# Sink attention and a folded feed-forward on one core: sink values by one full matmul, sink scores behind the score pairs, last tile in three parts

## The chip, the core and the metric

The kernel runs on one core of one Trainium2 chip. The metric is device time in microseconds (us), taken over the whole program. Three runs of the kernel before took 199.46, 199.68 and 200.15 us; their median is 199.68.

## What is computed

Four batches of eight heads, 768 positions, head width 64. Each position attends to the first four positions (the sink) and to a window of 128 positions that ends at itself. The result, as 3072 rows of 512, goes through a feed-forward layer in which two projections are multiplied.

```python
scores = scale * np.matmul(q, k.transpose(0, 1, 3, 2))
is_sink = pos[None, :] < n_sink                 # n_sink = 4
in_window = (rel >= 0) & (rel < window)         # window = 128
a = softmax(np.where(is_sink | in_window, scores, -1e9))
x = np.matmul(a, v).transpose(0, 2, 1, 3).reshape(B * S, H * D)
out = ((x @ w1) * (x @ w2)) @ w3 @ w_out        # 512 -> 1024 -> 1024 -> 512
```

## The kernel before

Everything is bf16 on TensorE, with sums in fp32. The product w3 @ w_out is formed once (`fold_w3`, `fold_mm`, lines 399 to 441), so that each row of output costs the two gate projections and one projection with the folded matrix.

**Attention.** Queries and keys must stand with the head width on the partitions. Batches 0 and 1 get that from TensorE (`transposes`, line 195, the tile `tp`, evacuated by DVE); batches 2 and 3 from transposing transfers that SP issues (`transposes_dma`, line 205). A head pair r and a stage t (two blocks of 128 queries, t = 0, 1, 2) make a unit: `scores` (line 250, tile `sc`) runs four or six matmuls of 64 rows, two heads beside each other on the array; ACT takes the exponential (line 261), DVE multiplies by the window's mask (line 265), and `values` (line 330, tile `av`) runs full-array matmuls with the masked weights as stationary operand. Its last column is the row sum, which DVE divides by (lines 350 and 353). Units are issued in pairs, since the second one of a pair is asked for first thing behind the lead. Batch 0 has units by block in its first two stages (`block_scores`, `block_values`). The results are transposed into `xT` by TensorE (tile `xt`) for batches 0 and 1, and by SP's transfers for 2 and 3.

**The sink.** A query block far from the start still needs the four sink positions. `sink_keys` (line 210) puts the four keys of each head into a block-diagonal operand `ksbd`, so that all eight heads' sink scores come out of four matmuls that each use 32 columns of the array (`sink_scores`, line 232, tile `sp`, once for each batch and each of the stages 1 and 2); ACT writes their exponentials to `es`. `sink_values` (line 222) brings the four sink rows of v to rows 32 * (h // 2) + 4 * (h % 2) of `vs`, so that one matmul for each head pair and block adds the sink's part to `av`. It does so with eight matmuls, one for each head, of four contraction rows each and 64 columns; the stationary operand is a shifted piece of a wide identity matrix, `shifts`. ACT evacuates the result (line 229).

**Feed-forward.** `gate` (line 379, tile `pg`) runs four matmuls for w1 (half 0, evacuated by ACT to `a_sb`) and four for w2 (half 1, multiplied by `a_sb` on DVE into `ab`), for chunks of 256 tokens in batch 0 and of 384 in the others. `project` (line 443, tile `po`) runs eight matmuls for 128 tokens, ACT copies the result (line 451), and SP writes it out (line 454). The very last tile is cut into two halves of 256 columns, the second of which ACT writes itself.

**What sets the order.** The order on TensorE, ACT, DVE and SP is written out while the program is built. Every piece of work is a task with a priority, an estimated time on each engine, the tasks that must be done or begun ahead of it, and the loads that it needs (lines 510 to 642). A planner (lines 645 to 763) keeps an estimated clock for each engine. At each step it takes for TensorE the task that can start first, and among those that can start at once the one of lowest priority number; the other engines take what is ready first. Score pairs are paced: the next may not start until `PACE[b]` us behind the one before (line 649). Where the planner sees TensorE idle early on, it puts in warming matmuls (`keep_busy`, line 457). Once the program is built the order is fixed; an instruction that is not ready holds up its engine. Tiles in PSUM come from two pools, two slots for scores and four for the rest. Loads of q, k and v are issued by POOL in a fixed order, at most eight at a time, and cast to bf16 on their way.

Of the kernel before, what the change touches and what calls it, by code (L numbers as in the profile page):

```python
# [21 lines left out]
def kernel(  # L22
# [31 lines left out]
    XPOSE = (2, 3)  # L54
    BLOCKS = ((0, 0), (0, 1))
    X_XPOSE = (2, 3)
    SPLIT = 6
# [9 lines left out]

    IPAD = P - 4
# [96 lines left out]
    nc.vector.memset(idle[:], 0.0)  # L165
    nc.vector.memset(shifts[:], 1.0)
    nc.vector.memset(maskt[:], 1.0)
    for b in range(B - 1):
        nc.vector.memset(ksbd[b][:], 0.0)

    nc.gpsimd.affine_select(shifts[:], shifts[:], compare_op=ALU.is_equal, fill=0.0,
                            base=-IPAD, pattern=[[1, IPAD + P]], channel_multiplier=-1)

# [43 lines left out]

    def sink_row(h):

        return 32 * (h // 2) + 4 * (h % 2)  # L220

    def sink_values(b):

        vp = ps_mm.tile([P, H, D], FP32, tag="mm", name="vp")
        for h in range(H):
            nc.tensor.matmul(vp[:, h, :], shifts[0:4, IPAD - sink_row(h):IPAD - sink_row(h) + P], vN[b][0:4, 0, h, 0:D],  # L226
                             start=(h == 0), stop=(h == H - 1))
        yield
        nc.scalar.copy(vs[b][:, :, 0:D], vp[:])
        yield  # L230

    def sink_scores(b, t):

        sp = ps_mm.tile([P, 256], FP32, tag="mm", name="sp")
        for r in range(NP):
            rows = slice(32 * r, 32 * r + 32)
            nc.tensor.matmul(sp[rows, :], ksbd[b][:, r * P + 32 * r:r * P + 32 * r + 32],  # L237
                             qT[b][:, r, t * 256:(t + 1) * 256], start=True, stop=True)
        yield
        nc.scalar.activation(es[b][:, (t - 1) * 256:t * 256], sp[:], ACTF.Exp, scale=scale)  # L240
        yield


# [199 lines left out]
    def project(b, m, n0, n1):  # L443

        po = ps_mm.tile([P, n1 - n0], FP32, tag="mm", name="po")
        for kk in range(KFF):
            nc.tensor.matmul(po[:], ab[b][:, kk, m * P:(m + 1) * P], w3o[:, kk, n0:n1],  # L447
                             start=(kk == 0), stop=(kk == KFF - 1))
        yield
        o_sb = w3_sb[:, (b * NB + m) % KFF, 2 * n0:2 * n1].bitcast(FP32)  # L450
        nc.scalar.copy(o_sb, po[:])  # L451
        yield
        t0 = b * S + m * P
        (nc.scalar if n0 else nc.sync).dma_start(out=out[t0:t0 + P, n0:n1], in_=o_sb)
        yield
# [73 lines left out]
    for i in range(KFF):  # L529
        for h in range(2):  # L530
            j0, j1 = 4 * h, 4 * h + 4
            needs = [need("w3", i, x) for x in range(j0 // 4, j1 // 4)]
            task(("t3", i, h), 100 + i + (5 if i < SPLIT and h else 0), fold_w3(i, j0, j1),
                 [("pe", 0.055 * (j1 - j0)), ("dve", 0.05 + 0.075 * (j1 - j0))],
                 [x for a, _ in needs for x in a], [x for _, a in needs for x in a],
                 started=[("t3", i, 0)] if i >= SPLIT and h else [folded(i - SPLIT)] if i >= SPLIT else [], ring="mm")
# [16 lines left out]
    for b in range(B):  # L553
        for t in range(NT):
# [3 lines left out]
            for kb in kbs:  # L558
                if b in XPOSE:
                    for n, src, dst in (("k", kN[b], kT[b]), ("q", qN[b], qT[b])):  # L560
                        qk.append(("td" + n, b, kb))
                        task(qk[-1], 1, transposes_dma(src, dst, kb), [("sp", 1.4), ("dma", XP_US)],
                             war, [(n, b, kb)])
                else:
                    qk.append(("tpk", b, kb))
                    task(qk[-1], 1, transposes(b, kb), [("pe", 0.48), ("dve", 0.65)],
                         war, [("k", b, kb), ("q", b, kb)], "mm")
            if t == 0:
                task(("sk", b), 0, sink_keys(b), [("dve", 0.2)], [("sc", b, 1, 0)])
                task(("sv", b), 2, sink_values(b), [("pe", 0.3), ("act", 0.5)],  # L570
                     [("av", b - 2, NP - 1, NT - 1), ("av", b, 1, 0)] if b >= 2 else [], [("v", b, 0)], "mm")
            else:
                task(("ss", b, t), 2, sink_scores(b, t), [("pe", 0.25), ("act", 0.4)],
                     qk + [("sk", b)], ring="mm")
            if (b, t) in BLOCKS:
                parts = [(j, r0, r0 + 2, [2 * i + r0 // 2]) for i, j in enumerate(kbs) for r0 in (0, 2)]
                if t == 0:
                    parts = [(0, 0, NP, [0, 1])] + parts[2:]
                for u, (j, r0, r1, avs) in enumerate(parts):
                    task(("sc", b, u, t), 4, block_scores(b, j, r0, r1),  # L580
                         [("pe", 0.3), ("act", 1.05), ("dve", 0.7)],
                         [("tpk", b, kb) for kb in (j - 1, j) if kb >= 0], ring="sc", paced=True,
                         started=([unit[-1][0]] if unit else []) + (unit[-4][1] if len(unit) > 3 else []))
                    for a in avs:
                        task(("av", b, a, t), 3, block_values(b, j, 2 * (a % 2)),
                             [("pe", 0.15 if j == 0 else 0.29 if j == 1 else 0.37), ("dve", 0.55)],
                             [("sc", b, u, t)] + ([("ss", b, t), ("sv", b)] if t else []),
                             [("v", b, j)], "mm", last_av)
                        last_av = [("av", b, a, t)]
                    unit.append((("sc", b, u, t), [("av", b, a, t) for a in avs]))  # L590
                    if avs[-1] % 2:
                        task(("xt", b, 2 * (j % 2), t), 2.5, block_x_transposes(b, j),
                             [("pe", 0.24), ("act", 0.6)],
                             [("av", b, avs[-1] - 1, t), ("av", b, avs[-1], t)], [], "mm")
                continue
            for r in range(NP):
                after = list(qk)
                if b >= 2 and t == 0:
                    after.append(("g", b - 2, len(CHUNKS[b - 2]) - 1, KFF - 1, 1))
                lead = r % 2 == 0  # L600
                task(("sc", b, r, t), 4 if lead else 0, scores(b, r, t),
                     [("pe", 0.22), ("act", 0.83), ("dve", 0.58)] if t == 0 else
                     [("pe", 0.28), ("act", 1.05), ("dve", 0.7)], after, ring="sc",
                     slots=2 if lead else 1, paced=lead,
                     started=([unit[-1][0]] if unit else []) + (unit[-3][1] if lead and len(unit) > 3 else []))
                task(("av", b, r, t), 3, values(b, r, t),
                     [("pe", 0.2 if t == 0 else 0.37), ("dve", 0.55)],
                     [("sc", b, r, t)] + ([("ss", b, t), ("sv", b)] if t else []),
                     [("v", b, kb) for kb in kbs], "mm", last_av)
                last_av = [("av", b, r, t)]  # L610
                unit.append((("sc", b, r, t), last_av))
                if not lead and b not in X_XPOSE:
                    task(("xt", b, r - 1, t), 2.5, x_transposes(b, r - 1, t),
                         [("pe", 0.24), ("act", 0.6)],
                         [("av", b, r - 1, t), ("av", b, r, t)], [], "mm")
# [5 lines left out]
    for b in range(B):  # L621
        for c, (t0, t1) in enumerate(CHUNKS[b]):
            last_t = (t1 - 1) // 256
            us = 0.01 + 0.65 * (t1 - t0) / 384
            for dt in range(KFF):
# [10 lines left out]
            for m in range(t0 // P, t1 // P):  # L636
                for n0 in (0, DM // 2) if (b, m) == (B - 1, NB - 1) else (0,):
                    n1 = n0 + DM // 2 if (b, m) == (B - 1, NB - 1) else DM
                    task(("p", b, m) + ((n0,) if n0 else ()), 1300 + 200 * b + m + n0 / 1000,
                         project(b, m, n0, n1),  # L640
                         [("pe", 1.75 * (n1 - n0) / DM), ("act", 0.6 * (n1 - n0) / DM), ("act", 0.1) if n0 else ("sp", SP_US)],
                         [("g", b, c, KFF - 1, 1), *[folded(i) for i in range(KFF)]], ring="mm")
# [77 lines left out]
    while len(done) < len(tasks):  # L720
# [21 lines left out]
        if e == "pe":  # L742
# [55 lines left out]
```

## Time and profile before

| | |
|---|---|
| median of three runs | 199.68 us |
| the profiled execution, its time and its span | 200.22 us, 198.5 us |
| DVE, ACT and POOL, share of the span | 56%, 54%, 38% |
| gate matmuls (line 386), TensorE busy | 91.5 us |
| projection matmuls (line 447), TensorE busy | 42.9 us |
| sink scores (line 237), sink values (line 226), TensorE busy | 2.3 us, 1.6 us |
| granted TensorE clock | 1.000 |
| share of 16 DMA engines' span, POOL's queue and SP's queue | 88.5%, 37.7% |

A row of the chain of waits has the start in us from the beginning of the span, the length in us, the engine, the tile and line, and how many instructions were joined. A row of the groups has line, engine, operation, what is written and read with the shapes, then the count, then busy time in us and mean ns of one, then the idle time just before and what ended it. A row of DMA issues ends with the time from issue to landing in us. "PE" is TensorE's matmuls, "PEld" its weight loads, "SPq" and "ACTq" are transfers issued by SyncE and ScalarE.

### The profile page before, as it was taken

The numbers are of one execution on the slowest core, as the hardware profiler recorded it, in microseconds if no ns is written. First come the engines' busy times: TensorE is split into PE (matmuls) and PEld (weight loads), VectorE is DVE, ScalarE is ACT, GpSimd is POOL, SyncE is SP. The second block draws the span as 40 slices with busy tenths as digits, with TensorE's granted clock in tenths as the row PEclk, the third lists the DMA queues.
The fourth block names the chain that finished last, engine by engine and source line by source line (L and its number), as shares of the span: only waits on it lengthen the run. The fifth ranks groups of instructions, "written<-read, shape, count | busy, mean of one in ns | idle before, by whom it ended". The sixth has DMA issues, their size and how long they took to land.

```text
span 198.5 us, 4533 instructions
## 1 busy us (share of the span) xinstructions
PE 190.3 (96%) x1803; PEld 118.9 (60%) x1815; DVE 111.8 (56%) x262; ACT 107.8 (54%) x179; POOL 75.9 (38%) x102
## 2 busy tenths in 40 slices
PE   7799999989999999999999999999999999999993
PEld 2345566968875786675666656665664565654442
DVE  5544487845786767577668748777781044440000
ACT  2234658634756777975755576667652433333332
POOL 5189967669899962733573300000000000000000
PEclk9999999999999999999999999999999999999999
DMA  5999999999999999999999999950203510002333
GB/s 138 398 387 182 180 159 196 196 160 154 155 144 184 211 144 106 178 158 183 124 144 146 126 156 186 197 110 2 51 5 90 182 48 2 0 3 104 142 141 141
DMA packets 105301, 28.35 MB, mean 143 GB/s; under 512 B 95168, under 2 KB 99776, under 8 KB 105280
## 3 DMA queue, kind: packets, MB, share of 16 engines
q0 software_dynamic: 79648, 12.33, 88.5%
q1 hardware_dynamic: 25488, 15.60, 37.7%
q8 instruction: 14, 0.23, 0.5%
q10 hardware_dynamic: 144, 0.13, 0.2%
q14 instruction: 7, 0.06, 0.1%
HBM read 29.36 MB, written 6.29 MB: 180 GB/s over the span
## 4 chain that ended last, share of the span: by engine, by line
PE 76%; DMA 17%; POOL 4%; SPq 1%; issue 1%; ACT 0%
PE pg L386 39%; PE po L447 21%; DMA w_sb<-in_moe_w_dram 7%; PE av L346 6%; DMA qN<-in_q_dram 5%; PE sc L256 5%; DMA ab<-in_moe_w_dram 4%; PE tp L200 2%; POOL qN L108 1%; POOL vN L108 1%; PE xt L362 1%; SPq L155 1%; POOL kN L108 1%; PE sp L237 1%; PE vp L226 1%
## 5 line engine op out<-in xcount | busy, mean ns | idle before, releaser
L386 PE MATMUL pg<-xT,w_sb 128*128 128x384 bf16 (+1 forms) x576 | 91.5, 308 | 0.0
L386 PEld LDWEIGHTS <-w_sb 128*128 128x128 bf16 x576 | 53.0, 98 | 25.5 <-issue 1.7
L390 DVE TENSOR_TENSOR ab<-a_sb,pg 128x384 bf16<-128x384 f32 (+1 forms) x72 | 36.5, 507 | 32.7 <-PE pg L386 26.2
L393 ACT COPY a_sb<-pg 128x384 f32<-128x384 f32 (+1 forms) x72 | 32.0, 444 | 34.6 <-PE pg L386 17.0
L447 PE MATMUL po<-w3o,ab 128*128 128x512 bf16 (+1 forms) x192 | 42.9, 370 | 0.4
L261 ACT ACTIVATE ex<-sc 128x1024 bf16<-128x1024 f32 (+1 forms) x40 | 37.8, 964 | 6.0 <-PE sc L256 4.1
L447 PEld LDWEIGHTS <-ab 128*128 128x128 bf16 x200 | 19.1, 98 | 20.4 <-issue 0.5
L451 ACT COPY w_sb<-po 128x512 f32<-128x512 f32 (+1 forms) x25 | 14.2, 568 | 25.6 <-PE po L447 25.5
L108 POOL DMA_DIRECT2D qN<-in_q_dram x24 | 22.3, 928 | 14.5 <-DMA vN<-in_v_dram 12.5
L265 DVE TENSOR_TENSOR am<-ex,maskt 128x1024 bf16<-128x1024 bf16 (+1 forms) x40 | 25.6, 645 | 3.6 <-ACT ex L261 3.4
L108 POOL DMA_DIRECT2D kN<-in_k_dram x24 | 22.0, 916 | 7.5 <-DMA qN<-in_q_dram 5.2
L108 POOL DMA_DIRECT2D vN<-in_v_dram x24 | 22.1, 922 | 6.4 <-DMA kN<-in_k_dram 4.5
L353 DVE TENSOR_TENSOR xn<-av,rec 128x256 bf16<-128x256 f32 x40 | 17.0, 424 | 1.4
L346 PE MATMUL av<-vN,am 128*128 128x65 bf16 x296 | 16.8, 193 | 0.0
L346 PEld LDWEIGHTS <-am 128*128 128x128 bf16 x296 | 14.4, 97 | 2.8 <-issue 0.3
L350 DVE RECIPROCAL rec<-av 128x4 f32<-128x4 f32 x40 | 7.2, 179 | 10.7 <-PE av L346 10.4
L202 DVE COPY kqT<-tp 128x1024 bf16<-128x1024 bf16 x12 | 8.3, 690 | 6.3 <-PE tp L200 6.3
L256 PE MATMUL sc<-kqT 64*128 64x128 bf16 (+1 forms) x216 | 11.6, 238 | 0.0
L346 PE MATMUL av<-vs,es 128*128 128x130 bf16 x56 | 11.1, 221 | 0.0
L256 PEld LDWEIGHTS <-kqT 64*128 64x128 bf16 x216 | 6.9, 94 | 3.2 <-issue 2.2
L433 PE MATMUL ph<-wo_sb,w3t 128*128 128x512 bf16 x31 | 7.9, 379 | 0.9 <-ACT wo_sb L413 0.6
L281 ACT ACTIVATE ex<-sc 128x1024 bf16<-128x1024 f32 x7 | 7.1, 1035 | 2.1 <-PE sc L277 2.1
(68 smaller groups left out, 135.6 us busy)
## 6 DMA issues: line engine op xcount, KB each, us to landing
out_dram<-w_sb SPq DMA_DIRECT2D x23, 256.0 KB, 2.2
kN<-in_k_dram POOLq DMA_DIRECT2D x24, 128.0 KB, 7.7
qN<-in_q_dram POOLq DMA_DIRECT2D x24, 128.0 KB, 8.1
vN<-in_v_dram POOLq DMA_DIRECT2D x24, 128.0 KB, 8.0
w_sb<-in_moe_w_dram POOLq DMA_DIRECT2D x9, 256.0 KB, 8.4
ab<-in_moe_w_dram SPq DMA_DIRECT2D x3, 512.0 KB, 6.3
ab<-in_moe_w_out_dram SPq DMA_DIRECT2D x3, 512.0 KB, 7.2
kN<-in_moe_w_dram SPq DMA_DIRECT2D x1, 512.0 KB, 9.4
```

Of the source, the lines that this page charges most:

```text
L108: nc.gpsimd.dma_start(out=dst, in_=rows(src, b, kb))
L202: nc.vector.tensor_copy(kqT[b][:, :, :, kb * P:(kb + 1) * P], tp[:])
L256: nc.tensor.matmul(sc[:, e, c:c + n], kT[b][hp, r, kb * P:(kb + 1) * P], qT[b][hp, r, qb * P:qb * P + n], start=True, stop=True)
L261: nc.scalar.activation(ex[:, :, c0:], sc[:, :, c0:], ACTF.Exp, scale=scale)
L265: nc.vector.tensor_mul(am[:, :, c0:], ex[:, :, c0:], mk)
L346: nc.tensor.matmul(o, lhs, rhs, start=(n == 0), stop=(n == len(todo) - 1), skip_group_check=True)
L353: nc.vector.tensor_mul(xns[b, t][:, :, r, :, :], av[:, :, :, 0:D], rec[:].to_broadcast([P, 2, 2, D]))
L386: nc.tensor.matmul(pg[:], w_sb[:, kk, dt * P:(dt + 1) * P], xT[b][:, kk, tk], start=(kk == 0), stop=(kk == NP - 1))
L390: nc.vector.tensor_mul(ab[b][:, dt, tk], gate_a.pop((b, c, dt))[:], pg[:])
L393: nc.scalar.copy(a_sb[:], pg[:])
L447: nc.tensor.matmul(po[:], ab[b][:, kk, m * P:(m + 1) * P], w3o[:, kk, n0:n1], start=(kk == 0), stop=(kk == KFF - 1))
L451: nc.scalar.copy(o_sb, po[:])
```

## The change

Sink values: one matmul of 128 contraction rows and 512 columns with `pick`, a matrix that copies each of the four sink rows to the eight places of the heads, so that every place gets all heads; DVE then multiplies by `ones_s`, the mask that keeps each head's own four rows. `shifts` becomes a plain identity.

Sink scores: the task now has priority -1 and may start once the second unit of the stage's first score pair has begun. Batch 1 (`SINKS`) makes both stages' sink scores with one group of 512 columns. In the planner's estimates a change of the array's shape is priced (`TURN`), the times of tasks on TensorE are set anew, and the pace of batch 2 is 3.5 in place of 5 and of batch 3 5.5 in place of 4.5.

Last tile: three parts of 256, 128 and 128 columns. ACT copies the first and the last, DVE the middle one; SP writes the first two, ACT the last.

```diff
+    SINKS = (1,)
...
-    shifts = const.tile([P, IPAD + P], BF16, name="shifts")
-    ident = shifts[:, IPAD:IPAD + P]
+    ident = const.tile([P, P], BF16, name="ident")
+    pick = const.tile([P, P], BF16, name="pick")
...
+    pk = pick[:].rearrange("p (r x) -> p r x", x=32)
+    for e in range(2):
+        nc.gpsimd.tensor_copy(pk[:, :, 4 * e:4 * e + 4],
+                              ident[:, 0:4].rearrange("p (r s) -> p r s", r=1).to_broadcast([P, NP, 4]))
...
         vp = ps_mm.tile([P, H, D], FP32, tag="mm", name="vp")
-        for h in range(H):
-            nc.tensor.matmul(vp[:, h, :], shifts[0:4, IPAD - sink_row(h):IPAD - sink_row(h) + P], vN[b][0:4, 0, h, 0:D],
-                             start=(h == 0), stop=(h == H - 1))
-        yield
-        nc.scalar.copy(vs[b][:, :, 0:D], vp[:])
+        nc.tensor.matmul(vp[:], pick[:], vN[b][:, 0, :, 0:D], start=True, stop=True)
+        yield
+        nc.vector.tensor_mul(vs[b][:, :, 0:D], vp[:],
+                             ones_s[:].rearrange("p (h o) -> p h o", o=1).to_broadcast([P, H, D]))
...
-    def sink_scores(b, t):
+    def sink_scores(b, t0, t1):
-        sp = ps_mm.tile([P, 256], FP32, tag="mm", name="sp")
+        sp = ps_mm.tile([P, (t1 - t0) * 256], FP32, tag="mm", name="sp")
...
-                             qT[b][:, r, t * 256:(t + 1) * 256], start=True, stop=True)
+                             qT[b][:, r, t0 * 256:t1 * 256], start=True, stop=True)
...
-        nc.scalar.copy(o_sb, po[:])
+        (nc.vector.tensor_copy if n0 == DM // 2 else nc.scalar.copy)(o_sb, po[:])
...
-        (nc.scalar if n0 else nc.sync).dma_start(out=out[t0:t0 + P, n0:n1], in_=o_sb)
+        (nc.scalar if n0 > DM // 2 else nc.sync).dma_start(out=out[t0:t0 + P, n0:n1], in_=o_sb)
...
-                task(("ss", b, t), 2, sink_scores(b, t), [("pe", 0.25), ("act", 0.4)],
-                     qk + [("sk", b)], ring="mm")
+                if b not in SINKS:
+                    task(("ss", b, t), -1, sink_scores(b, t, t + 1), [("pe", 0.12), ("act", 0.4)],
+                         qk + [("sk", b)], ring="mm", started=[] if (b, t) in BLOCKS else [("sc", b, 1, t)])
+                elif t == 1:
+                    more = [(n, b, kb) for n in (("tdk", "tdq") if b in XPOSE else ("tpk",)) for kb in (4, 5)]
+                    task(("ss", b, 1), -1, sink_scores(b, 1, NT), [("pe", 0.225), ("act", 0.6)],
+                         qk + more + [("sk", b)], ring="mm", started=[("sc", b, 1, 1)])
...
-                for n0 in (0, DM // 2) if (b, m) == (B - 1, NB - 1) else (0,):
-                    n1 = n0 + DM // 2 if (b, m) == (B - 1, NB - 1) else DM
+                cuts = (0, DM // 2, 3 * DM // 4, DM) if (b, m) == (B - 1, NB - 1) else (0, DM)
+                for n0, n1 in zip(cuts, cuts[1:]):
...
-    PACE = [0.0, 3.4, 5, 4.5]
-    last_sc = 0.0
+    PACE = [0.0, 3.4, 3.5, 5.5]
+    TURN, SHAPE = 0.095, {"sc": 1, "ss": 2}
+    last_sc, shape = 0.0, 0
...
+            if SHAPE.get(k["name"][0], 0) != shape:
+                shape = SHAPE.get(k["name"][0], 0)
+                us += TURN
```

More of the change, by code (lines that the diff above doesn't have):

```diff
@@ L165 @@
     nc.vector.memset(idle[:], 0.0)
-    nc.vector.memset(shifts[:], 1.0)
+    nc.vector.memset(ident[:], 1.0)
     nc.vector.memset(maskt[:], 1.0)
+    nc.vector.memset(pick[:], 0.0)
     for b in range(B - 1):
         nc.vector.memset(ksbd[b][:], 0.0)
-    nc.gpsimd.affine_select(shifts[:], shifts[:], compare_op=ALU.is_equal, fill=0.0,
-                            base=-IPAD, pattern=[[1, IPAD + P]], channel_multiplier=-1)
+    nc.gpsimd.affine_select(ident[:], ident[:], compare_op=ALU.is_equal, fill=0.0,
+                            base=0, pattern=[[1, P]], channel_multiplier=-1)
     m4 = maskt[:].rearrange("p v (a c q) -> p (v a) c q", c=2, q=P)
@@ L237, in sink_scores @@
             nc.tensor.matmul(sp[rows, :], ksbd[b][:, r * P + 32 * r:r * P + 32 * r + 32],
-                             qT[b][:, r, t * 256:(t + 1) * 256], start=True, stop=True)
+                             qT[b][:, r, t0 * 256:t1 * 256], start=True, stop=True)
         yield
-        nc.scalar.activation(es[b][:, (t - 1) * 256:t * 256], sp[:], ACTF.Exp, scale=scale)
+        nc.scalar.activation(es[b][:, (t0 - 1) * 256:(t1 - 1) * 256], sp[:], ACTF.Exp, scale=scale)
         yield
@@ L565 @@
                     qk.append(("tpk", b, kb))
-                    task(qk[-1], 1, transposes(b, kb), [("pe", 0.48), ("dve", 0.65)],
+                    task(qk[-1], 1, transposes(b, kb), [("pe", 0.45), ("dve", 0.65)],
                          war, [("k", b, kb), ("q", b, kb)], "mm")
@@ L585 @@
                         task(("av", b, a, t), 3, block_values(b, j, 2 * (a % 2)),
-                             [("pe", 0.15 if j == 0 else 0.29 if j == 1 else 0.37), ("dve", 0.55)],
-                             [("sc", b, u, t)] + ([("ss", b, t), ("sv", b)] if t else []),
+                             [("pe", 0.125 if j == 0 else 0.245 if j == 1 else 0.36), ("dve", 0.55)],
+                             [("sc", b, u, t)] + ([("ss", b, 1 if b in SINKS else t), ("sv", b)] if t else []),
                              [("v", b, j)], "mm", last_av)
@@ L601 @@
                 task(("sc", b, r, t), 4 if lead else 0, scores(b, r, t),
-                     [("pe", 0.22), ("act", 0.83), ("dve", 0.58)] if t == 0 else
-                     [("pe", 0.28), ("act", 1.05), ("dve", 0.7)], after, ring="sc",
+                     [("pe", 0.17), ("act", 0.83), ("dve", 0.58)] if t == 0 else
+                     [("pe", 0.225), ("act", 1.05), ("dve", 0.7)], after, ring="sc",
                      slots=2 if lead else 1, paced=lead,
@@ L606 @@
                 task(("av", b, r, t), 3, values(b, r, t),
-                     [("pe", 0.2 if t == 0 else 0.37), ("dve", 0.55)],
-                     [("sc", b, r, t)] + ([("ss", b, t), ("sv", b)] if t else []),
+                     [("pe", 0.187 if t == 0 else 0.36), ("dve", 0.55)],
+                     [("sc", b, r, t)] + ([("ss", b, 1 if b in SINKS else t), ("sv", b)] if t else []),
                      [("v", b, kb) for kb in kbs], "mm", last_av)
@@ L623 @@
             last_t = (t1 - 1) // 256
-            us = 0.01 + 0.65 * (t1 - t0) / 384
+            us = 0.65 * (t1 - t0) / 384
             for dt in range(KFF):
```

16 lines of the change are left out of this document (7 added, 9 removed).

## Prediction

> **What bounds the kernel now.** I read, from coarse to fine, the page's engine totals, the chain that ended last in order of time, TensorE's timeline where the chain reaches it, and one window over the long stretch behind that.
>
> ```profile
> PE 190.3 (96%) x1803; PEld 118.9 (60%) x1815; DVE 111.8 (56%) x262; ACT 107.8 (54%) x179; POOL 75.9 (38%) x102
> ...
> 33.70 10.39 DMA qN<-in_q_dram
> ...
> 195.34 0.37 ACT w_sb L451
> ```
>
> ```profile
> 43.37 0.40 PE L200 MATMUL tp<-shifts,kN 128*128 128x128 bf16 x4 [0.23 <-DMA kN<-in_k_dram]
> 44.14 0.40 PE L200 MATMUL tp<-shifts,qN 128*128 128x128 bf16 x4 [0.38 <-DMA qN<-in_q_dram]
> ...
> 44.14:195.34 151.20, 150.75 (x1416) 94.83 (x1424) 84.86 (x198) 85.33 (x146) 45.31 (x54) 1.00 1.21 120
> ```
>
> The last row's columns are length, then busy time of PE, PEld, DVE, ACT and POOL, then granted clock. The reader should see two regimes. Up to 44.14 us the chain is a transfer: the queries of batch 0, block 4, land at 33.70 + 10.39 = 44.09 us and TensorE transposes them at once. From 44.14 to 195.34 us it is TensorE alone, busy 150.75 of 151.20 us at full clock, with DVE and ACT a little over half busy. In that stretch a microsecond of matmul time taken out is a microsecond of kernel, as long as nothing else becomes late. Ahead of 44.14 it is worth nothing.
>
> Where TensorE loses time inside the stretch shows when equal groups are compared by what ran before them:
>
> ```profile
> 62.23 1.73 PE po L447 x8
> ...
> 64.40 0.22 PE sp L237 x4
> ...
> 91.89 0.44 PE sc L256 x8
> 92.33 0.22 PE sp L237 x4
> 92.55 0.76 PE pg L386 x4
> 93.31 0.34 PE vp L226 x8
> 93.64 1.41 PE pg L386 x8
> ...
> 100.98 0.65 PE pg L386 x4
> ```
>
> Four gate matmuls take 0.65 us behind a full-array group (100.98), but 0.76 behind the sink scores, and eight take 1.41 instead of 1.30 behind the sink values. Each return to the full array thus costs 0.11 us. Going the other way costs about the same: eight 64-column matmuls of the sink values stream 512 columns, which at 1.73/8 = 0.216 us per 512 columns would be 0.22, and take 0.34. A sink-score group takes 0.22 both behind a score pair (92.33) and behind a full group (64.40), so a switch between two partial shapes costs what any other switch costs. A partial-shape group standing alone pays two switches; one directly behind a score pair adds only one.
>
> **The change part by part.** I counted groups and shapes in the order in which each kernel issues to TensorE. Behind the queries at 44.14 us both issue the same score, value, gate and transpose groups; what differs in work is:
>
> *Sink values*, three of the four in the stretch. Before: 0.34 + 0.11 for the return = 0.45 us. After: one full-array matmul of 512 columns, 0.216 (the po row, same shape). 3 x 0.234 = **0.70 us** less.
>
> *Sink scores of batch 1*, two groups standing alone, 2 x (0.22 + 0.11) = 0.66 us. After: one group of 512 columns behind a pair, whose return to the full array it takes over: 0.11 for the switch plus 0.22 for streaming (a 256-column group streams 0.22 - 0.11 = 0.11). **0.33 us** less. The trace has no 32-column matmul of 512 columns; bounds are 0.22 (no dearer than now) and 0.44 (two of now). I take 0.33, which is streaming doubled and the switch once.
>
> *Sink scores of batches 2 and 3*: four groups, of which one already stands behind a pair (92.33). Three move behind one: 3 x 0.11 = **0.33 us**. Batch 0's stood ahead of its pair and moves behind it: nothing. In all 58 switches become 46.
>
> *The evacuation of the sink values* goes from ACT to DVE as a multiplication by the head mask.
>
> ```profile
> L229 ACT CAST vs<-vp 128x512 bf16<-128x512 f32 x4 | 2.4, 590 | 2.2 <-PE vp L226 2.2
> L353 DVE TENSOR_TENSOR xn<-av,rec 128x256 bf16<-128x256 f32 x40 | 17.0, 424 | 1.4
> L390 DVE TENSOR_TENSOR ab<-a_sb,pg 128x384 bf16<-128x384 f32 x48 | 26.5, 553 | 27.6 <-PE pg L386 22.5 <-ACT ex L261 3.0 <-ACT a_sb L393 0.7
> ```
>
> ACT sheds 0.59 us four times. DVE pays between 0.55 (384 wide) and 0.85 (twice 424 ns); along the slope of these rows, 0.13 per 128 columns, 512 wide is 0.69. TensorE covers it while DVE has room; the squeeze is a rival below. The constants (one more memset on DVE, two small copies on POOL) stand ahead of POOL's wait for a weight transfer:
>
> ```profile
> POOL spent L190 <- DMA ab<-in_moe_w_dram: 5.4, 1, 5.4
> ```
>
> POOL sits idle there for 5.4 us, so the start of the loads does not move.
>
> *The front.* Ahead of the transposes at 43.4 us TensorE gets 0.43 us more work: one more warming matmul (0.22), four more switches because two score pairs are split (0.44), less 0.23 for the first sink values. TensorE waits 0.23 + 0.38 = 0.61 us there today, so this is hidden; without that cover it costs 0.43.
>
> *The tail.* The last tile goes out as 256, 128 and 128 columns.
>
> ```profile
> 194.51 0.37 ACT L451 COPY w_sb<-po 128x256 f32<-128x256 f32 x1 [0.29 <-PE po L447]
> 195.75 0.37 ACTq L454 DMA_DIRECT2D out_dram<-w_sb  x1
> ...
> out_dram<-w_sb ACTq DMA_DIRECT2D x1, 128.0 KB, 1.7
> ...
> out_dram<-w_sb SPq DMA_DIRECT2D x3, 256.0 KB, 2.0
> L451 ACT COPY w_sb<-po 128x512 f32<-128x512 f32 x23 | 13.5, 585 | 24.8 <-PE po L447 24.7
> 61.38 0.45 PE tp L200 x8
> ```
>
> The copy falls by 0.21 us from 512 to 256 columns, so 128 columns should take 0.27: 0.10 less. The write falls by 0.3 from 256 to 128 KB; halving again should give 0.15, bounded by 0 and 0.3. Eight 128-column matmuls take 0.45 (61.38); two such pieces take 0.90 in place of the 0.83 between the two copies: 0.07 more. The middle piece is copied by DVE and issued by SP 0.45 us earlier than the last, so the last one still ends the kernel. Net **0.18 us** less. The Trainium skill (DMA: Bandwidth & Descriptors, Anatomy of one DMA) says that about 2.0 us of a transfer is fixed and does not scale with size. By that the smaller write gains nothing and the tail gives 0.03; the two rows above differ by 0.3 with size, so I keep 0.15.
>
> **Sum**: 0.70 + 0.33 + 0.33 + 0.18 = 1.54 us. The profiled execution took 200.22 us, 198.5 of span and 1.7 around it; the sum makes 198.7 of it. The median of the runs shown is 199.68, 0.54 lower, and becomes 198.14.
>
> **Forecast: 198.1 us**, by itself 197.6 to 198.7.
>
> **The rivals.** The new plan moves more than the sink work. With the pace of batch 2 cut from 5 to 3.5, its attention runs earlier, and that is where covers can fail.
>
> *A transfer takes the place (slower).* The first score pair of batch 2's last third needs the query block that SP transposes last:
>
> ```profile
> 108.53 0.55 PE sc L256 x12
> ...
> 77.61 0.88 POOL L108 DMA_DIRECT2D qN<-in_q_dram  x1 [3.08 <-DMA vN<-in_v_dram]
> qN<-in_q_dram POOLq DMA_DIRECT2D x1, 128.0 KB, 14.1
> ...
> 77.63 0.33 SPq L454 DMA_DIRECT2D out_dram<-w_sb  x1
> ...
> 90.24 1.19 SPq L207 DMA_TRANSPOSE kqT<-kN  x1
> kqT<-kN SPq DMA_TRANSPOSE x1, 7.1
> 91.77 1.19 SPq L207 DMA_TRANSPOSE kqT<-qN  x1
> kqT<-qN SPq DMA_TRANSPOSE x1, 8.5
> DMA to landing us min/median/max: 3.6/8.4/10.9
> ```
>
> It lands at 91.77 + 8.5 = 100.3 us; today TensorE comes for it at 108.5, 8 us later. After, nine gate groups (5.85), one value group (0.36), nine switches (0.99) and 0.14 of streams less stand ahead of it: 108.5 - 7.3 = 101.2. The cover shrinks to 0.9 us. Against this: it is still cover, and SP's transposes are issued earlier too, since the output that goes out at 77.63, ahead of a query transpose on SP's queue, is computed 10 us sooner. For it: those outputs and transposes now compete earlier with the load, which itself took 14.1 us. With the longest transpose of 10.9 it lands at 102.7, a wait of 1.5: 199.7, the gain gone. One more transfer ahead of the load costs the spacing of the two transposes, 100.3 - 97.3 = 3.0: landing at 103.3, wait 2.1, 200.3; both together 105.7, wait 4.5, 202.7. It decides against the change from a landing at 102.7. The Trainium skill (same page, Queues, rings and completion order) has each DMA engine serve its queue rows in turn, packet by packet. By that rule early SP transfers do slow POOL's loads, which is this rival's mechanism; this trace shows only the long landings.
>
> *An engine takes the place.* In batch 0's last third the first two score pairs come closer:
>
> ```profile
> 49.14 0.55 PE sc L256 x12
> ...
> 53.23 0.44 PE pg L386 x4
> 53.66 0.55 PE sc L256 x12
> ...
> L261 ACT ACTIVATE ex<-sc 128x1024 bf16<-128x1024 f32 x28 | 28.1, 1028 | 4.2 <-PE sc L256 3.7 <-DVE rec L350 0.5
> L265 DVE TENSOR_TENSOR am<-ex,maskt 128x1024 bf16<-128x1024 bf16 x28 | 19.0, 685 | 2.2 <-ACT ex L261 2.0
> L202 DVE COPY kqT<-tp 128x1024 bf16<-128x1024 bf16 x12 | 8.3, 690 | 6.3 <-PE tp L200 6.3
> L240 ACT ACTIVATE es<-sp 128x256 bf16<-128x256 f32 x8 | 3.1, 384 | 1.3 <-PE sp L237 1.1
> ```
>
> Today 4.5 us lie between them; after, one pair, the sink scores, four gate groups, a transpose group and the sink values: 0.55 + 0.22 + (4 x 0.44 + 0.11) + 0.45 + 0.22 = 3.3. ACT needs 2 x 1.03 + 0.38 + 2 x 0.37 (gate copies of 256 columns, priced as the half tile's) = 3.2 in it; DVE needs 2 x 0.69 for the masks, 0.69 for the transposes and 0.69 for the sink values, 2.8, and a gate product or two. Both are full. Against it: the consumers of these pairs stand 4 to 10 us behind them. Batch 2's first pairs are as close (3.5 to 3.9 us). Some 0.3 us at one place to 0.4 at three: 198.5 to 199.4, mid 198.9.
>
> *The change does not do what it says*: if the mask multiply and the wide group hold TensorE as switches did, only the shorter streams and the tail remain, 0.3 us: 199.4.
>
> **How the numbers follow.** A measurement of this kernel tells 0.3%, 0.6 us, from no change: faster means under 199.1, slower over 200.3. Forecast 0.50 (faster). Engine squeeze 0.17: 0.12 faster, 0.05 same. Transfer late but within the gain (199.1 to 200.3) 0.13, same. Transfer later than that, 200.3 to 202.7: 0.13, slower. No effect 0.07, same. Faster 0.62, same 0.25, slower 0.13. The range runs from 197.6 (tail write and wide group at their good ends, 0.26, and the scatter of the runs, which reached 0.2 under their median) to 200.2; the slower rival and some low end, about 0.17, stay outside.
>
> **What would show it.** Right: gate groups behind score pairs with sink scores still at 0.76, none behind the sink values above 0.65; 149.9 us from the query transposes of block 4 to the last copy (151.2 - 1.36 + 0.07); that copy at 0.27. Wrong: an idle row of TensorE released by a key or query transpose near 101 us (first rival), or by ACT or DVE near 50 or 88 us (second); the query transposes of block 4 clearly after 44.2 us (front); a 512-column sink-score group at 0.44.

## The result and the profile after

The changed kernel takes 198.76 us, the kernel before 199.82 (medians of 21 and 22 runs): a ratio of 0.9946, 95% interval 0.9923 to 0.9970. That is 1.1 us less, between 0.6 and 1.5. A second set of runs, told below, gives 0.9918 (0.9892 to 0.9944), or 1.6 us less, between 1.1 and 2.2. The forecast of 198.1 us stood for 1.54 us less. The profiled execution of the changed kernel took 198.11 us with a span of 196.4. Runs over 1.5% longer than the fastest of their kernel, at a granted clock of 0.982 to 0.992, are left out of the medians here and below: one of the changed kernel (203.12 us), one with four more loads (206.49), one with the new estimates (204.38).

The page's engine totals of the changed kernel:

```profile
PE 189.7 (97%) x1778; PEld 119.2 (61%) x1792; DVE 115.0 (59%) x268; ACT 104.9 (53%) x174; POOL 76.0 (39%) x104
```

Over the whole span TensorE has 0.6 us less to do than before, ACT 2.9 us less and DVE 3.2 us more. Now the same long stretch, from the query transposes of block 4 to the last copy, as a window over the changed kernel (length, then busy time of PE, PEld, DVE, ACT and POOL, then granted clock):

```profile
43.45:193.53 150.08, 149.51 (x1397) 94.37 (x1407) 87.05 (x203) 83.33 (x142) 45.49 (x54) 1.00 1.20 121
```

150.08 us in place of 151.20, and TensorE is busy for 149.51 of it in place of 150.75. The two spans differ by 2.1 us: 0.69 ahead of the stretch (43.45 against 44.14), 1.12 in it, and 0.3 behind the start of the last copy (196.4 - 193.53 = 2.9, before 198.5 - 195.34 = 3.2). The two medians differ by 1.1 only. The first of the three parts varies by nearly as much, 0.6 us, between two executions of the kernel before (the last experiment), so it is not counted as the change's here.

Next the places in the chain of waits of the changed kernel that answer to the ones shown of before (start, length, what ran):

```profile
67.39 0.55 PE sc L255 x12
67.94 0.33 PE sp L237 x4
68.27 0.54 PE pg L385 x4
...
90.08 0.22 PE vp L226
90.29 1.30 PE pg L385 x8
91.59 0.55 PE sc L255 x12
92.14 0.22 PE sp L237 x4
92.36 0.76 PE pg L385 x4
...
100.70 0.55 PE sc L255 x12
101.25 0.22 PE sp L237 x4
...
193.53 0.27 ACT w_sb L450
```

The sink values (90.08) take 0.22 us and the eight gate matmuls behind them 1.30: both switches are gone. Sink scores stand directly behind score pairs, and the gate group behind them still pays the one return, 0.76 in place of 0.65 (92.36). The wide sink-score group of batch 1 takes 0.33 (67.94), as forecast; its return is paid by the group behind it, whose matmuls have 256 columns: 0.54 in place of the 0.44 that four such matmuls take. The multiplication that DVE took over, in the groups of the changed kernel by form:

```profile
L228 DVE TENSOR_TENSOR vs<-vp,ones_s 128x512 bf16<-128x512 f32 x4 | 2.8, 690 | 0.3 <-PE vp L226 0.2
```

0.690 us each, where the slope had given 0.69.

### The profile page after: what moved, and what is told of

It is laid out like the page before. It is cut to its first block, busy times and chain, and to the rows that moved or that the text cites. A ratio compares the mean times of both kernels' runs of the same rounds, so it can differ in the third digit from the quotient of the medians.

```text
span 196.4 us, 4491 instructions
## 1 busy us (share of the span) xinstructions
PE 189.7 (97%) x1778; PEld 119.2 (61%) x1792; DVE 115.0 (59%) x268; ACT 104.9 (53%) x174; POOL 76.0 (39%) x104
## 4 chain that ended last, share of the span: by engine, by line
PE 85%; DMA 8%; POOL 4%; SPq 1%; issue 1%; DVE 0%; ACT 0%
PE pg L385 43%; PE po L446 21%; PE av L345 7%; PE sc L255 5%; DMA ab<-in_moe_w_dram 4%; DMA w_sb<-in_moe_w_dram 4%; PE tp L205 3%; PE pw L432 2%; POOL qN L108 1%; PE xt L361 1%; POOL vN L108 1%; PE av L308 1%; SPq L155 1%; POOL kN L108 1%; PE sp L237 1%; PE sc L276 1%
## 5 line engine op out<-in xcount | busy, mean ns | idle before, releaser
L446 PE MATMUL po<-w3o,ab 128*128 128x512 bf16 (+2 forms) x198 | 42.6, 362 | 0.5
L450 ACT COPY w_sb<-po 128x512 f32<-128x512 f32 (+2 forms) x25 | 14.1, 566 | 25.9 <-PE po L446 24.0
```

Of the source, the lines that this page charges most:

```text
L450: (nc.vector.tensor_copy if n0 == DM // 2 else nc.scalar.copy)(o_sb, po[:])
```

## The experiments

Two theories. **Switches**: the time comes from 12 changes of the array's shape that are gone, at 0.11 us each, some streaming, and a shorter tail. **Plan**: the time comes from the new order and pace, whatever the array's shapes. Beside them stand the two rivals of the prediction, a late transfer and a full DVE. "Before" and "after" are the two kernels. Each group of runs was timed against the kernel before on the same chip (medians 200.1 to 200.4 us).

### Sink values by eight matmuls again, all of full height

Edit of after, from which the cost of the number of matmuls is read:

```diff
-        nc.tensor.matmul(vp[:], pick[:], vN[b][:, 0, :, 0:D], start=True, stop=True)
+        for h in range(H):
+            nc.tensor.matmul(vp[:, h, :], pick[:], vN[b][:, 0, h, 0:D], start=(h == 0), stop=(h == H - 1))
```

> The changed kernel, but the sink values again by eight matmuls of 64 columns, now each with all 128 contraction rows. Theory (the change of the array's shape is what cost): the same 512 columns stream at full shape, 0.22 to 0.29 us for each batch, the gate matmuls behind take 0.65 and not 0.76, 46 switches, and the stretch from the query transposes of block 4 to the last copy stays at 150.1 to 150.3 us. Rival (the number of matmuls is what cost): 0.45 us for each batch again, the stretch 150.8.

Measured: 198.42 us, ratio 0.9912 (0.9878 to 0.9946). Its chain of waits:

```profile
88.99 1.30 PE pg L386 x8
90.29 0.23 PE vp L227 x8
90.53 1.30 PE pg L386 x8
```

Eight matmuls cost 0.01 us more than one, and the group behind them is not delayed. It is not the number. The stretch is 150.57 us where 150.1 to 150.3 was expected. The order on TensorE is that of after, so the two timelines can be laid beside each other: TensorE came early here (block 4's queries at 43.17) and waited twice for loads of q and v, 0.28 us at 46.57 and 0.28 at 50.15, against one wait of 0.13 at 59.5 in after. At the sink values stand 0.01 us each.

### Sink values by one matmul of four rows

Edit of after, the other half of the old form:

```diff
-        nc.tensor.matmul(vp[:], pick[:], vN[b][:, 0, :, 0:D], start=True, stop=True)
+        nc.tensor.matmul(vp[:], pick[0:4, :], vN[b][0:4, 0, :, 0:D], start=True, stop=True)
```

> The changed kernel, but its one 512-column matmul of the sink values uses four contraction rows only. Theory (shape): 0.33 us for each batch and 0.11 more for what follows, 52 switches, the stretch 150.7 us. Rival (number of matmuls): as the changed kernel, 0.22 and 150.1.

Measured: 199.40 us, ratio 0.9945 (0.9909 to 0.9981). Its chain of waits:

```profile
88.64 1.30 PE pg L385 x8
89.95 0.32 PE vp L226
90.26 1.41 PE pg L385 x8
```

One matmul of the same 512 columns with four contraction rows takes 0.32 and makes the next group 1.41: 0.10 going in and 0.11 coming out. The shape costs, in both directions, even where only the height differs. The interval can't tell this kernel from after; the rows can. Beside after, start by start in the same order, TensorE loses 0.20 us at each of the three sink values in the stretch, 0.59 in all, and doesn't have the wait of 0.13 at 59.5. That gives 150.08 + 0.59 - 0.13 = 150.54, and the stretch is 150.55 (150.7 was expected). The Trainium skill (TensorEngine Tiling (Array Packing), Key Properties) says that a change of tiling mode drains TensorE, and gives no price. The trace agrees in so far as each change of the rows or columns in use costs 0.10 to 0.11 us here; that it is a drain, and that four rows count as a mode of their own, it does not show.

### The old pace

Edit of after:

```diff
-    PACE = [0.0, 3.4, 3.5, 5.5]
+    PACE = [0.0, 3.4, 5, 4.5]
```

> The changed kernel with the paces of before (5 and 4.5): batch 2's third pair of stages comes 6 us later. Theory: the new order of batches 2 and 3 is worth nothing by itself, the stretch stays at 150.1 us and the time within 0.3% of the changed kernel (198.2 to 199.3). Rival (the re-planned order gives part of the gain): the stretch goes back towards 151.2, the time towards 199.8.

Measured: 198.69 us, ratio 0.9929 (0.9903 to 0.9954), the stretch 150.06 us as in after. With the new estimates the new pace brings nothing over the old one, so the order of batch 2 is not where the time came from.

### Four more loads ahead of batch 2's last blocks

Edit of after. The loads fill tiles that nothing reads; all else is computed.

```diff
+    extra = [const.tile([P, DM], BF16, name=f"extra{i}") for i in range(4)]
...
+                if (i[0], kb) == (2, 5):
+                    for x in extra:
+                        nc.gpsimd.dma_start(out=heads(x[:]), in_=rows(v, 2, 4))
```

> The changed kernel with four more loads of 128 KB (the values of batch 2, block 4, into tiles that nothing reads) ahead of the loads of batch 2, block 5. It prices the transfer rival. In the changed kernel the last query block of batch 2 lands 3.4 us ahead of TensorE. If that is the cover, four loads of 1.2 to 1.5 us each make it land 5 to 6 us later, TensorE waits 1.5 to 2.5 us for it near 100.7 us and perhaps once more for batch 3: 200.2 to 201.5. With the cover of 0.9 us that the forecast gave this rival: a wait of 4 to 5 us, 203. If these transfers are no bound at all: 198.8.

Measured: 202.22 us, ratio 1.0110 (1.0062 to 1.0158), more than the 200.2 to 201.5 that was expected. SyncE issues the transposing transfer of the query block at 96.80 (its timeline), it takes 7.9 us, and TensorE's timeline shows who is waiting:

```profile
96.80 2.27 SPq L216 DMA_TRANSPOSE kqT<-qN  x1
```

```profile
104.75 0.56 PE L259 MATMUL sc<-kqT 64*128 64x256 bf16 x10 [2.96 <-DMA kqT<-qN]
```

A late landing does cost TensorE its time: 96.80 + 7.9 = 104.7, and TensorE stands for 2.96 us. That earlier transfers of SyncE's would make the load late, which was the prediction's reason, is not shown by this edit. In after the same transfer is issued at 89.75 and takes 7.5:

```profile
89.75 1.32 SPq L212 DMA_TRANSPOSE kqT<-qN  x1
```

It lands at 97.3, 3.4 us ahead of the score pair at 100.70. The landing here is 7.4 us later, where 5 to 6 was expected. That would cost 4.0; it cost 2.96, since TensorE here came 1.1 us later to that point (104.75 - 2.96 = 101.8).

### The last tile alone

Before, with the last tile in three parts (the change's lines in `project` and in the cuts) and nothing else.

> The kernel before with the three-part last tile alone. Theory (shape switches make the stretch, the tail is a separate small gain): 58 switches, the stretch from the query transposes of block 4 to the last copy as before, 151.2 us, and 2.87 in place of 3.18 us from the last copy to the end. Rival (a transfer's cost is fixed, so a smaller last write gains nothing): 3.08 us behind the last copy, only the copy being shorter. Its front is that of the kernel before, so it also shows when those queries land there in one more execution: between 43.2 and 44.4 us if that only scatters, about 44.1 if the order of before made them late.

Measured: 200.34 us, ratio 1.0015 (0.9993 to 1.0036). The end of its timeline:

```profile
195.43 0.29 DVE L451 COPY w_sb<-po 128x128 f32<-128x128 f32 x1 [16.29 <-ACT w_sb L451]
195.79 0.41 SPq L454 DMA_DIRECT2D out_dram<-w_sb  x1
195.82 0.27 ACT L451 COPY w_sb<-po 128x128 f32<-128x128 f32 x1 [0.48 <-PE po L447]
196.12 0.37 ACTq L454 DMA_DIRECT2D out_dram<-w_sb  x1
```

From the last copy to the end are 198.7 - 195.82 = 2.9 us, 0.3 less than before, and the stretch is 151.23. So the part does in the trace what it should, some 0.3 us less. In the runs it can't be seen: the interval reaches down to 0.9993, that is 0.14 us less. Why they show less than the trace stays open; the front, where the queries of block 4 landed at 44.55 in this execution, later than either theory expected, is one candidate.

### The sink values alone

Before, with the changed `sink_values`, `pick` and that task's own estimates.

> The kernel before with the sink values by one full-array matmul and the mask on VectorE alone; paces, sink scores and tail as before. Theory: 52 switches in the stretch, three batches at 0.23 us less, the stretch 150.5 us. Rival (the planner's new order makes the gain): the stretch stays at 151.2.

Measured: 199.97 us, ratio 0.9977 (0.9961 to 0.9994); the stretch 151.75 us where 150.5 was expected. The expectation failed. TensorE's timeline of this kernel:

```profile
57.18 0.39 PE L206 MATMUL tp<-shifts,kN 128*128 128x128 bf16 x4
57.84 0.34 PE L206 MATMUL tp<-shifts,qN 128*128 128x128 bf16 x3 [0.28 <-DMA qN<-in_q_dram]
```

From one start to the next are 0.66 us, and four transposes take 0.22: TensorE waited 0.44 us for a load. (The idle time in brackets is shorter, since it counts from a modelled end; a wait is read better from start to start.) Besides, four gate matmuls (0.44) that before runs ahead of block 4's transposes run behind them here, so the stretch begins with more to do. That leaves 150.9. Two shorter waits make up most of the other 0.4. The group of four gate matmuls at 49.66 is followed by the sink values at 50.26, after 0.60 us in place of 0.44, and the view of waits names a load of v; the sink values at 94.86 are followed by gate matmuls at 95.24, after 0.38 in place of 0.22, and it names DVE's division (line 358).

### The sink scores alone

Before, with the changed `sink_scores`, `SINKS`, and those tasks' priorities and estimates.

> The kernel before with the sink scores behind the score pairs and one wide group for batch 1 alone; paces, sink values and tail as before. Theory: 52 switches, the stretch 150.55 us (0.66 less), the wide group at 0.33 us. Rival (the planner's new order): 151.2.

Measured: 200.36 us, ratio 1.0014 (0.9993 to 1.0034); the stretch 151.48 where 150.55 was expected. TensorE's timeline:

```profile
82.52 0.29 PE L362 MATMUL xt<-shifts,xn 128*128 128x128 bf16 x2
82.97 0.28 PE L362 MATMUL xt<-shifts,xn 128*128 128x128 bf16 x2 [0.16 <-DVE xn L353]
83.09 0.49 PE L386 MATMUL pg<-xT,w_sb 128*128 128x384 bf16 x2
83.96 0.49 PE L386 MATMUL pg<-xT,w_sb 128*128 128x384 bf16 x2 [0.38 <-ACT xT L366]
```

Two transposes take 0.11 (four take 0.22), and 0.45 lie between the starts: 0.34 waited for DVE. Two gate matmuls take 0.33 (four 0.65), and 0.87 lie between: 0.54 waited for ACT's copy of those transposes. Without these 0.88 us the stretch is 150.6, the expected figure. The switches went as they should, and a new wait of an attention result took the time back.

### The mask multiplication three times

Edit of after: the multiplication is done three times over, 1.38 us more on DVE for each batch.

```diff
+        for _ in range(3):
-        nc.vector.tensor_mul(vs[b][:, :, 0:D], vp[:],
+            nc.vector.tensor_mul(vs[b][:, :, 0:D], vp[:],
```

> The changed kernel with the mask multiplication of the sink values made three times, 1.38 us more of VectorE for each batch at the same place. Theory (VectorE has room, and TensorE meets its consumers late enough): the stretch stays at 150.1 us. Rival (the engine squeeze of the forecast): each batch's sink values hold back the masks and gate products behind them, TensorE waits for VectorE near 51 us and 91 us, 0.4 to 1.4 us at each of three places, the stretch 151 to 153.

Measured: 200.91 us, ratio 1.0060 (1.0029 to 1.0091); the stretch 152.45. TensorE's waits in it (us in total, how often, the longest):

```profile
PE av L346 <- DVE am L265: 1.1, 2, 0.8
PE pg L386 <- DVE vs L229: 0.4, 1, 0.4
```

The rival's expectation came true. The value matmuls wait for the window's masks near 54 and 95 us, some us behind the places (50 and 88) where the prediction had looked for the squeeze, and gate matmuls wait near 127. DVE has not 1.4 us to spare there. It has 0.69: after shows no such row.

### The whole change with the old estimates

In the traces the two parts alone lost their gain to waits that after doesn't have. After differs from their sum by the planner's estimates. So: after, with the estimates, the paces and the missing switch price of before (some lines):

```diff
-            us = 0.65 * (t1 - t0) / 384
+            us = 0.01 + 0.65 * (t1 - t0) / 384
...
-                     [("pe", 0.225), ("act", 1.05), ("dve", 0.7)], after, ring="sc",
+                     [("pe", 0.28), ("act", 1.05), ("dve", 0.7)], after, ring="sc",
...
-            if SHAPE.get(k["name"][0], 0) != shape:
-                shape = SHAPE.get(k["name"][0], 0)
-                us += TURN
```

> The whole change with the planner's estimates, paces and no price of a switch, as in the kernel before; the order on TensorE is then another one, with the same 46 changes of shape behind the query transposes of block 4. Theory that the new estimates keep the work free of waits: TensorE waits for 0.4 to 1.0 us inside the stretch, as in the two parts alone, the stretch is 150.6 to 151.2 us, the ratio to the kernel before 0.997 to 1.000. Rival that the estimates are worth nothing and the parts add up: no wait, stretch 150.1 us, ratio 0.993 to 0.995 as for the whole change.

Measured: 199.25 us, ratio 0.9948 (0.9928 to 0.9967). TensorE's timeline:

```profile
81.18 0.29 PE L361 MATMUL xt<-ident,xn 128*128 128x128 bf16 x2
81.62 0.28 PE L361 MATMUL xt<-ident,xn 128*128 128x128 bf16 x2 [0.16 <-DVE xn L352]
81.75 0.49 PE L385 MATMUL pg<-xT,w_sb 128*128 128x384 bf16 x2
82.62 0.32 PE L385 MATMUL pg<-xT,w_sb 128*128 128x384 bf16 x1 [0.39 <-ACT xT L365]
```

The same wait as with the sink scores alone, 0.33 + 0.54 = 0.87 us; its stretch is 151.09, without the wait 150.2. So the new figures (estimates, pace and switch price together) are worth about 0.9 us to the new operations in the trace. The ratio came out lower than that theory had expected (0.997 to 1.000) and fits the rival's 0.993 to 0.995, so the times show less of it than the trace; against after itself, timed beside it below, the medians differ by 0.6 us, and the two intervals overlap.

### The new estimates with the old operations

Before, with after's estimates of common work, its paces and its switch price, and the operations untouched.

> The kernel before, its operations untouched, with the new estimates, paces and the price of a switch: 55 changes of shape in place of 58. If the estimates by themselves bring time, the stretch falls from 151.2 to 150.9 us or less and the ratio is 0.997 to 0.999. If they only fit the new operations, the stretch stays at 151.2 or grows by new waits, ratio 1.000 to 1.004.

Measured: 200.84 us, ratio 1.0022 (0.9993 to 1.0050); the stretch 151.29. The estimates alone bring no time. TensorE's timeline shows why:

```profile
122.48 0.40 PE L226 MATMUL vp<-vN,shifts 4*128 4x64 bf16 x8
123.22 0.29 PE L237 MATMUL sp<-kqT,ksbd 128*32 128x256 bf16 x4 [0.34 <-ACT ex L261]
```

Three changes of shape fewer are worth 0.33 us. From the sink values to the sink scores are 0.74 us, for 0.22 of streaming and one change of 0.11: a new wait of 0.41 takes them back. In these two experiments the estimates pay only together with the operations that they describe.

### After, once more

No edit.

> The changed kernel once more, as the measure for the other two on the same chip. By the switch theory the stretch is 150.1 us in this execution too, whatever the landing of block 4's queries, which sets the front (43.2 to 44.7 us so far). The cover of batch 2's query block varies: the theory that the profiled pair's 0.7 us of front is scatter expects queries to land anywhere in that range and the ratio at 0.993 to 0.996; the rival that the change also advances the front expects them below 43.6 again and a ratio of 0.990 or less.

Measured: 198.62 us, ratio 0.9918 (0.9892 to 0.9944); the stretch 150.50, from 43.13 to 193.63. The stretch was expected at 150.1 and is 0.42 longer than in the first execution. TensorE's timeline has it:

```profile
45.99 0.39 PE L205 MATMUL tp<-ident,kN 128*128 128x128 bf16 x4
46.42 0.28 PE L205 MATMUL tp<-ident,qN 128*128 128x128 bf16 x2
...
49.50 0.39 PE L205 MATMUL tp<-ident,qN 128*128 128x128 bf16 x4
50.01 0.39 PE L226 MATMUL vp<-vN,pick 128*128 128x512 bf16 x1
```

Four transposes of 0.22 take 0.43 and 0.51 here: TensorE came early and waited 0.21 + 0.29 us for the next loads. The second of them is a load of v. An early front is given back at the loads behind it. The queries landed at 43.09, below 43.6 as the rival had it; the ratio lies between what the two theories expected. In the first execution of after one such place is left as well (59.18 to 59.53, with 0.22 to do):

```profile
59.18 0.38 PE L205 MATMUL tp<-ident,kN 128*128 128x128 bf16 x4
59.53 0.34 PE L205 MATMUL tp<-ident,qN 128*128 128x128 bf16 x3
```

### Before, once more

No edit.

> The kernel before, once more, timed against itself: the ratio should be 1.000 and its interval shows what this measurement can tell. Theory that the front of the two profiled executions differs by scatter: the queries of block 4 land anywhere from 43.1 to 44.7 us, and the stretch behind them is 151.2 us and the end behind the last copy 3.17 us as in the first execution, whatever the front. Rival that the kernel before is always late in front: they land at 44.0 us or later once more.

Measured: 200.16 us, ratio 0.9994 (0.9976 to 1.0011). This is what the measurement tells of two equal kernels. The load of block 4's queries, in POOL's timeline:

```profile
34.01 0.88 POOL L108 DMA_DIRECT2D qN<-in_q_dram  x1 [0.49 <-DMA w_sb<-in_moe_w_dram]
```

It took 9.5 us and landed at 43.5, in the first execution of the same kernel at 44.09, so before is not always late. Over the eight executions of after and the kernels made from it this load landed between 43.1 and 44.4, at 43.6 in the mean; over the six of before's kind between 43.5 and 44.7, at 44.2 in the mean. The 0.69 us by which the front differed in the first pair of profiles can be scatter, which is 1.2 to 1.3 us wide within each kind. That the change also advances this landing by some tenths is not ruled out by 14 executions. The stretch and the tail don't depend on it.

The stretch was 152.08 us, 0.9 longer than in the first execution, and not the 151.2 expected. SyncE's timeline and TensorE's:

```profile
93.29 1.19 SPq L207 DMA_TRANSPOSE kqT<-qN  x1
```

```profile
101.17 0.28 PE L346 MATMUL av<-vN,am 128*128 128x65 bf16 x4
101.84 0.29 PE L237 MATMUL sp<-kqT,ksbd 128*32 128x256 bf16 x4 [0.39 <-DMA kqT<-qN]
...
124.32 0.36 PE L346 MATMUL av<-vN,am 128*128 128x65 bf16 x6
124.92 0.29 PE L237 MATMUL sp<-kqT,ksbd 128*32 128x256 bf16 x4 [0.25 <-DVE rec L350]
```

The transposed query block of batch 2 landed 8.4 us after its issue, at 101.7, and the **sink scores** stood waiting for it: 0.67 us from one start to the next, where the first execution takes 0.22 (four value matmuls, 0.12, and the change of shape). These 0.45 us are the transfer rival's mechanism, in the kernel before. Another 0.31 were lost ahead of the sink scores at 124.92 (0.60 in place of 0.29), which the view puts down to VectorE's reciprocal.

## Why the prediction was right, step by step

**The bound.** Right, with one correction. Behind 44.14 us TensorE sets the time; but up to about 59.5 us the loads are only tenths of a microsecond ahead of it. In after the transposes at 59.53 start 0.05 us behind the landing of their load, and in its second execution so do the groups at 46.42 and 50.01. What the change saves ahead of 59.5 (the sink values of batch 1, 0.23) can be given back there.

**Sink values, 0.70, and sink scores, 0.66.** The sizes hold. The stretch should have fallen by 1.36 - 0.07 = 1.29 to 149.9; it fell by 1.12 to 150.08, and without the 0.13 us of waiting at 59.18 it is 149.95. The count holds: the traces have 58 changes of shape in the stretch of before and 46 in that of after. The reason holds too: the switch and not the number of matmuls or their columns. The wide group, bounded by 0.22 and 0.44, took the 0.33 that was chosen.

**The evacuation by DVE, 0.69 and hidden.** Right in price and in cover; three of them don't fit.

**The tail, 0.18.** Right in sign, too small: 0.3 less behind the start of the last copy, and between the two copies of ACT 0.85 us in place of 0.83, so 0.02 more where 0.07 was forecast. That makes 0.28. The copy is the 0.27 that was forecast. In the issues of transfers of the changed kernel the last write is

```profile
out_dram<-w_sb ACTq DMA_DIRECT2D x1, 64.0 KB, 1.6
```

against 1.7 before with 128 KB. The fall of 0.3 that the prediction halved stood between a write that SyncE issues and one that ScalarE issues; on SyncE alone the last writes of the two kernels take 2.0, 1.8 and 1.7 us for 256, 128 and 64 KB. The Trainium skill (DMA: Bandwidth & Descriptors, Anatomy of one DMA) gives about 2.0 us that do not scale with size for a transfer that GpSimd issues, and beside it a part that grows with the bytes. So "gains nothing" did not follow from it; and the smaller writes here, which GpSimd does not issue, stay below 2.0 us in all.

**The front.** The 0.43 us of added work stayed hidden, as said. That after came 0.69 earlier there was not forecast; how much of it is scatter is open, as told above.

**The transfer rival.** It did not decide, but the step that priced it failed. "Today TensorE comes for it at 108.5, 8 us later" looked at the first score pair only. The sink scores need the same query block, and stand ahead of that pair. The chain of before:

```profile
101.63 0.36 PE av L346 x10
101.99 0.22 PE sp L237 x4
102.21 0.76 PE pg L386 x4
```

So the cover today is 101.99 - 100.3 = 1.7 us, not 8. The change puts the sink scores behind the pair and the pair at 100.70 (101.2 was forecast), and covers it by 3.4 us in one execution and, with the block landing at 99.9 and the pair at 100.80, by 0.9 in the other. The change did not open this risk; it was there, and the second execution of before paid 0.45 us for it. With covers from 0.9 to 3.4 us, that no landing struck in after's two profiled executions is in part luck.

**The squeeze rival.** It did not come about in after; with three multiplications it came about near the places named. **The change doing nothing** is out: after's rows at 90.08 and 90.29 and the two edits of the sink values speak against it.

**The sum.** 1.54 us lies at the edge of the first interval (0.6 to 1.5) and well inside the second (1.1 to 2.2). The traces, without the front, give 1.12 + 0.3 = 1.4. The measured 198.76 lies 0.6 above the forecast. The two sets of runs, 1.1 and 1.6 us less, scatter too much to say how much of this the sum had wrong.

**What the prediction did not see** is what holds the sum together. It took the order of after as given, and that this order brings no new wait was no step of its working. With the old estimates the same operations run into a wait of 0.87 us for an attention result near 82 us. So a good part of the change's worth hangs on figures in a planner: 0.87 of 1.4 us in the traces, 0.6 of 1.75 in the medians of that set of runs. Which of the new figures removes the wait wasn't tried; the pace alone is not it.

## What to carry to other kernels

Count changes of the array's shape as work, at 0.11 us each here, a matmul with few rows among them; give such work full-array operands of zeros and mask it on an engine with room, or put it next to a group that already pays. When operations get cheaper, set the planner's estimates anew in the same edit and look for waits of tenths of a microsecond, from start to start. To price the cover of a transfer, find the first reader of its data among all readers, not the largest one.

## What the runs showed of the hardware that was not expected

The same load in the same program lands 0.6 us apart in two executions (44.09 and 43.5), and over the 14 executions of all kernels here 1.6 us apart, with no difference in its issue of more than 1 us. A transposing transfer of a query block takes 7.5 to 8.6 us from issue to landing in five executions, of which SyncE's issue is 1.2 to 2.3. In the profiled executions the mean clock granted to TensorE is 0.998 or more, and in each of them 1.00 over the stretch that is compared, so none of the differences between traces come from it.
